# Linear attention and a gated convolution MoE on one core: keys' maximum as a bias in batch 0 only, later ranks for weights and MoE, other buffer counts, and six products on a zeroed tile first

## The chip, the cores and the metric

The kernel runs on one core of a Trainium2 chip. The metric is the device time of one execution in microseconds (us), the median of several runs. The core has five engines, each with its own list of instructions that it works off in order: TensorE (PE for products, PEld for the loads of their weights), VectorE (DVE), ScalarE (ACT), GpSimd (POOL) and SyncE (SP), which here issues every DMA. They wait for each other by semaphores alone.

## The reference

Eight batches with eight heads of 576 rows and 64 columns. Attention is linear: keys and queries are projected to 128 features, less the row's largest absolute value, and taken as exp(+) and exp(-). Its output, 512 wide for each row, goes through one feed-forward part with a convolution of three taps as gate.

```python
def phi(x):
    proj = np.einsum('bhsd,df->bhsf', x, w_phi)
    proj = proj - np.max(np.abs(proj), axis=-1, keepdims=True)
    return np.concatenate([np.exp(proj), np.exp(-proj)], axis=-1)
q_p, k_p = (phi(q), phi(k))
kv = np.einsum('bhsf,bhsd->bhfd', k_p, v)
z = np.sum(k_p, axis=2)
num = np.einsum('bhsf,bhfd->bhsd', q_p, kv)
den = np.einsum('bhsf,bhf->bhs', q_p, z)[..., None] + 1e-06
...
h = np.maximum(x @ w_in, 0.0)
...
gate = 1.0 / (1.0 + np.exp(-conv_out))
return (h * gate @ w_out).astype(np.float32)
```

Here x is the attention's output, w_in is 512 x 1024, w_out 1024 x 512, and conv_out the convolution of h along the rows. The three MoE weights come as float64.

## The kernel before

**Work and tiles.** Two heads lie side by side on the partitions, so a batch has two halves `qd` of four heads, each cut into five groups `g`: four of 256 columns for a pair of heads (n = 2, four row blocks of 128 in the end) and a short one for the last 64 rows of all four heads (n = 1). There are 80 key groups (`k_group`, line 418) and 80 query groups (`q_group`, line 460). Numbers that must keep float32's accuracy are split into a high and a low part in a faster format, and a product is made of three: high by high, high by low, low by high. The projections of batch 0's queries and of three key groups use plain float32 instead (`plain`, line 373).

**A key group.** `project` (line 370) loads it, splits it on POOL, projects it on PE into PSUM, and DVE takes the largest absolute value for each row and head block (line 404). For keys, ACT makes the negated maximum (line 407), and eight exponentials of 128 columns each read PSUM with the maximum, or its negative, as a bias (line 427; four in the short group). PE multiplies them with the values into `kv` (lines 441 and 445), in small tiles of 64 columns.

**A query group.** Here DVE subtracts the maximum from the whole group (line 411) into the SBUF tile `qs`, PE transposes it (line 469), ACT takes two exponentials of 512 columns (line 474), PE multiplies them by `kv` in small tiles (line 489), and DVE divides: the tile `x` (line 501).

**MoE.** Each pair of batches is cut into three chunks of 384 rows, twelve in all. `x_part` (line 509) transposes x and splits it, `h_part` (line 546) makes 8 blocks of h with 12 products each (line 562), relu on ACT, the convolution on POOL and DVE (lines 567 and 574) into the one tile `c`, the sigmoid, the gate's product (line 582) and its split into `gh` and `gl` (lines 591 and 594). `o_part` (line 598) makes four output blocks of 24 products (line 612). Chunk 0 needs the eight x tiles of batch 0 (g = 1 to 4 in both halves), chunk 1 four of them again, a short one of each half and four of batch 1, chunk 2 all of batch 1.

**Weights.** `load_weight` (line 340) loads a 128 x 512 piece of float64 words and rounds it by hand: in `float64_round` four DVE steps (lines 301, 306, 309, 316), two ACT steps (304, 313) and a POOL product (320), then a cast on ACT (362) and the low part on POOL (363). There are eight pieces of w_in, then eight of w_out. The raw words sit in the two slots `gh`, the half-made ones in the two slots `gl`, the same slots that the gate's tiles take later. Slots of a kind are given out in the order in which the program names their tiles, so every weight comes before the first gate tile. The first four blocks of h need pieces 0, 2, 4 and 6, which come first.

**The order.** A planner (`Plan`, line 88) writes the five lists. Each piece of work has an engine, a planned cost and hold, a rank, and the tiles that it reads, writes and takes. `order` (line 158) goes through planned time: it takes the work that can start earliest, and among those that can start at the same time the lowest rank. Work that needs a slot which isn't free can't start. Products in small tiles (`tiled`) are held back while PE has other work until four of them (`NT`) stand ready or one has waited 12 us; once PE has turned to them, it goes on with all that are ready.

**Ranks.** The chains are numbered: ten key groups of batch 0, then a query group of batch b and a key group of batch b+1 by turns, 160 in all. A key or query group has its number as its rank. Weight j of w_in has WIN0 + WIN x j, of w_out WOUT0 + WOUT x j, its DMA three less. Chunk n has M0 + 12.5 n + LEAD, that is 30 + 12.5 n.

**Buffers.** KE tiles of exponentials of keys (two per group), QE of queries (one per group), NXX tiles x of long groups (and four for the short ones), QS for `qs`, NHH for h. PSUM has four banks for general use, two (`M`) for h and output blocks (and batch 0's keys), two for `kv`.

Of the kernel before, what the change touches and what calls it, by code (L numbers as in the profile page):

```python
# [7 lines left out]
F32 = mybir.dt.float32  # L8
# [3 lines left out]
AF = mybir.ActivationFunctionType  # L12
# [4 lines left out]
F = 128  # L17
DM, FF = 512, 1024
P = 128
# [18 lines left out]
SWITCH = (120, 250)  # L38
TABLE = 1283
PSUM_G = 4  # L40
LEAD = 20
WIN0 = 0.0
WIN = 2.5
WOUT0 = 20.0
WOUT = 3.0
AGE = 12000.0
NT = 4
SLACK = 0.0
# [1 line left out]
RX = 0.0  # L50
OL = 0.0
KPLAIN = 3
KE = 6
NXX = 12
NHH = 10
TR = 2
QS = 2
QE = 3
V = 3
OS = 2  # L60
KVF = 6
# [165 lines left out]
def kernel(  # L227
# [13 lines left out]
    nc = tc.nc  # L241
# [6 lines left out]
    def piece(shape, dtype, name, tag, n=1):  # L248
        return Piece(sb, shape, dtype, name, [f"{tag}_{i}" for i in range(n)])

    def const(shape, dtype, name):
        return Piece(cp, shape, dtype, name, [name])

    G = [f"g_{i}" for i in range(PSUM_G)]
    M = [f"m_{i}" for i in range(2)]

    def psum(shape, name, slots):
        return Piece(pg, shape, F32, name, slots, True)
# [8 lines left out]
    def act(cost, hold, emit, reads, writes, rank, takes=(), table=None):  # L267
        plan.add("ACT", cost, hold, emit, reads, writes, rank, takes, table=table)

    def pool(cost, hold, emit, reads, writes, rank, takes=()):  # L270
        plan.add("POOL", cost, hold, emit, reads, writes, rank, takes)

    def mm(cost, emit, reads, writes, rank, takes=(), tiled=False):
        plan.add("PE", cost, cost, emit, reads, writes, rank, takes, tiled=tiled)

    def w_(*ps):
        return [p if isinstance(p, tuple) else (p, None) for p in ps]
# [11 lines left out]
    bias_e = const([P, 1], F32, "bias_e")  # L289
    pool(99, 60, lambda: nc.gpsimd.memset(bias_e(), -896.0 * (1 << 23)), (), w_(bias_e), -30)  # L290

    def float64_round(raw, w, power, n, rank, rraw, rw, rpower):


        def words():
            v = raw().rearrange("p (n two) -> p n two", two=2)
            return v[:, :, 0], v[:, :, 1]

        big = n > 100
        tcost = (700, 620) if big else (170, 95)  # L300
        vec(*tcost, lambda: nc.vector.tensor_scalar(out=w().bitcast(I32), in0=words()[1], scalar1=0x7FF00000, scalar2=None,
                                             op0=ALU.bitwise_and), rraw, rw, rank)
        act(*((722, 620) if big else (297, 190)),
            lambda: nc.scalar.activation(out=power().bitcast(I32), in_=w().bitcast(I32), func=AF.Relu, scale=8.0,
                                         bias=bias_e()), rw + w_(bias_e), rpower, rank + 0.01)
        vec(*tcost, lambda: nc.vector.tensor_scalar(out=w().bitcast(I32), in0=words()[1], scalar1=0xFFFFF, scalar2=0x100000,
                                             op0=ALU.bitwise_and, op1=ALU.bitwise_or), rraw, rw, rank + 0.02)
        vec(*((900, 820) if big else (700, 620)),
            lambda: nc.vector.scalar_tensor_tensor(out=power().bitcast(I32), in0=words()[1], scalar=-2147483648,
                                                   in1=power().bitcast(I32), op0=ALU.bitwise_and,  # L310
                                                   op1=ALU.bitwise_or), rraw + rpower, rpower, rank + 0.03)
        act(*((677, 570) if big else (210, 116)),
            lambda: nc.scalar.activation(out=words()[0].bitcast(F32), in_=words()[0].bitcast(U32), func=AF.Copy,
                                         scale=2.0**-52), rraw, [(p, "low") for p, _ in rraw], rank + 0.03)
        vec(*((930, 850) if big else (170, 95)),
            lambda: nc.vector.scalar_tensor_tensor(out=w(), in0=w().bitcast(I32), scalar=2.0**-20,
                                                   in1=words()[0].bitcast(F32), op0=ALU.mult, op1=ALU.add),
            rw + [(p, "low") for p, _ in rraw], rw, rank + 0.04)
        pool(*((1350, 1250) if big else (238, 200)),
             lambda: nc.gpsimd.tensor_tensor(out=w(), in0=w(), in1=power(), op=ALU.mult), rw + rpower, rw, rank + 0.05)  # L320
# [49 lines left out]
    def project(src, b, qd, g, kind, r):  # L370
        c0, n = group_columns(g)
        nm = f"{b}_{qd}_{g}"
        plain = kind == "q" and 2 * b + qd < NQ_F32 or kind == "k" and b == 0 and 5 * qd + g < KPLAIN
        raw = piece([P, n * P], F32, f"{kind}r{nm}", "th" if plain else "tr", TH if plain else TR)
        dma(lambda: raw(), lambda: src[b, qd, :, c0 : c0 + n * P], 64 * n, r - 3.0, writes=w_(raw))
        if not plain:
            hi = piece([P, n * P], F32R, f"{kind}xh{nm}", "th", TH)
            lo = piece([P, n * P], F32R, f"{kind}xl{nm}", "tl", TL)
            pool(*((407, 371) if n == 2 else (300, 265)),
                 lambda: nc.gpsimd.tensor_scalar(out=hi(), in0=raw(), scalar1=1.0, scalar2=0.0, op0=ALU.mult,  # L380
                                                 op1=ALU.add), w_(raw), w_(hi), r - 1.5)
            pool(*((735, 695) if n == 2 else (458, 420)),
                 lambda: nc.gpsimd.tensor_tensor(out=lo(), in0=raw(), in1=hi().bitcast(F32), op=ALU.subtract),  # L383
                 w_(raw, hi), w_(lo), r - 1.5)
        ps = psum([P, n * 256], f"{kind}p{nm}", M + G if b == 0 and kind == "k" else G)
        m = piece([P, 2, 2 * n], F32, f"{kind}m{nm}", "m", 6)
        pr = None if kind == "k" else piece([P, 2 * n, F], F32, f"qs{nm}", "qs", QS)

        def emit():
            for t in range(n):  # L390
                o = ps()[:, t * 256 : (t + 1) * 256]
                if plain:
                    nc.tensor.matmul(out=o, lhsT=raw()[:, t * P : (t + 1) * P], rhs=wbd_f(), start=True, stop=True)
                    continue
                his, los = hi()[:, t * P : (t + 1) * P], lo()[:, t * P : (t + 1) * P]
                nc.tensor.matmul(out=o, lhsT=his, rhs=wbd_hi(), start=True, stop=False)  # L396
                nc.tensor.matmul(out=o, lhsT=his, rhs=wbd_lo(), start=False, stop=False)  # L397
                nc.tensor.matmul(out=o, lhsT=los, rhs=wbd_hi(), start=False, stop=True)  # L398

        mm((432 if plain else 357) * n, emit, w_(raw, wbd_f) if plain else w_(hi, lo, wbd_hi, wbd_lo), w_(ps), r,  # L400
           takes=(m,) if pr is None else (m, pr))
        ps3 = lambda: ps().rearrange("p (t f) -> p t f", f=F)
        vec(*((690, 600) if n == 2 else (415, 331)),
            lambda: nc.vector.tensor_reduce(out=m()[:, 0], in_=ps3(), axis=AX, op=ALU.max, apply_absolute_value=True),  # L404
            w_(ps), [(m, 0)], r)
        if pr is None:
            act(200, 60, lambda: nc.scalar.activation(out=m()[:, 1], in_=m()[:, 0], func=AF.Copy, scale=-1.0), [(m, 0)],
                [(m, 1)], r)
            return n, ps, m
        vec(*((690, 600) if n == 2 else (415, 331)),  # L410
            lambda: nc.vector.tensor_tensor(out=pr(), in0=ps3(),
                                            in1=m()[:, 0].unsqueeze(2).broadcast_to([P, 2 * n, F]), op=ALU.subtract),
            [(ps, None), (m, 0)], w_(pr), r - 0.1)
        return n, pr

    kvps, kv = {}, {}

    def k_group(b, qd, g, r):
        n, ps, m = project(kT, b, qd, g, "k", r)
        nm = f"{b}_{qd}_{g}"  # L420
# [2 lines left out]
        dma(lambda: v(), lambda: vt[b, qd, :, v0 * VW : (v0 + 4) * VW], 130, r - 1.0, writes=w_(v))  # L423
        e = [piece([P, 2 * n, F], F32, f"ke{nm}_{s}", "ke", KE) for s in range(2)]
        for s in (1, 0):
            for i in range(2 * n):
                act(277, 160, lambda s=s, i=i: nc.scalar.activation(  # L427
                    out=e[s]()[:, i], in_=ps()[:, i * F : (i + 1) * F], func=AF.Exp, scale=1.0 - 2.0 * s,
                    bias=m()[:, 1 - s, i : i + 1]), [(ps, None), (m, 1 - s)], [(e[s], i)], r, table="Exp")
        if g == 0:  # L430
# [201 lines left out]
    for j, n in enumerate((0, 2, 4, 6, 1, 3, 5, 7)):  # L632
        load_weight(n, WIN0 + WIN * j)
    for j in range(8):
        load_weight(8 + j, WOUT0 + WOUT * j)
    rank_of = {}
# [5 lines left out]
    for n in range(NCH):  # L642
        r = M0 + step * n + LEAD
        x_part(n, r + RX)
        h_part(n, r)
        if n > 0:
            o_part(n - 1, r + 4.5 + OL)
    o_part(NCH - 1, M0 + step * NCH + LEAD + 4.5)

# [59 lines left out]
```

## Time and profile before

| what | us |
|---|---|
| median of 3 runs (lowest to highest) | 784.03 (783.07 to 784.82) |
| the profiled execution's own time | 784.47 |
| its span, first to last instruction | 782.7 |
| PE busy in the span | 751.4 |
| DVE, ACT, POOL busy | 500.2, 461.1, 286.3 |
| first product on PE starts | 5.81 |

The page gives for each engine the busy time, then the span in 40 equal slices with the busy share of each in tenths. The windows give the same for stretches that are chosen. The groups put together the instructions of one line, engine and operation: their tiles, how many, their busy time, the mean time of one, and the idle time before them. Products on PE overlap, so that their busy time hides how close they follow each other; the timeline gives the starts. The chain of waits goes back from the last instruction to what released each step.

### The profile page before, as it was taken

What the parts mean: (1) busy time and instruction counts of PE and PEld (TensorE: products, weight loads), DVE (VectorE), ACT (ScalarE), POOL (GpSimd) and SP (SyncE); (2) the same over time, 40 slices, a digit from 0 to 9 for tenths busy, and PEclk for the clock granted to TensorE, in tenths of its full rate; (3) what the DMA queues carried; (4) which work ended last, traced back from release to release, by engine and by line L of the source; (5) the groups of instructions that cost most, each with busy time, mean ns of one, the idle gap of its engine ahead of it and who ended that gap; (6) DMA issues with size and microseconds to landing.
All of it is one profiled execution on the core that took longest, in us unless ns stands there. A gap on an engine that the chain in (4) does not pass through costs nothing.

```text
span 782.7 us, 20365 instructions
## 1 busy us (share of the span) xinstructions
PE 751.4 (96%) x8265; PEld 720.7 (92%) x8265; DVE 500.2 (64%) x1030; ACT 461.1 (59%) x1172; POOL 286.3 (37%) x428
## 2 busy tenths in 40 slices
PE   6888888999999999999999999999999999999998
PEld 5777887899999999999999999999999999999997
DVE  4898788755566655666756665666555757766550
ACT  6998748665547727646647654736654763733341
POOL 4877675422252412433512341423332434220110
PEclk9999999999999999999999999999999999999999
DMA  5655311112202311220311221201310220000001
GB/s 176 198 154 153 108 56 45 48 32 75 72 21 58 86 38 46 69 56 32 89 33 56 58 62 35 79 22 35 107 43 25 85 70 21 29 12 22 21 21 50
DMA packets 46604, 48.88 MB, mean 62 GB/s; under 512 B 5296, under 2 KB 44464, under 8 KB 46512
## 3 DMA queue, kind: packets, MB, share of 16 engines
q1 hardware_dynamic: 46512, 47.59, 20.6%
q8 instruction: 65, 1.06, 0.6%
q14 instruction: 27, 0.22, 0.1%
HBM read 38.13 MB, written 9.44 MB: 61 GB/s over the span
## 4 chain that ended last, share of the span: by engine, by line
PE 76%; ACT 11%; DVE 9%; POOL 2%; issue 1%; DMA 1%; SPq 0%; POOLq 0%; ACTq 0%
PE hp L562 24%; PE op L612 23%; PE nm L489 8%; ACT ke L427 6%; PE kv L445 6%; PE tp L469 4%; PE xt L532 2%; DVE c L574 2%; PE qp L396 2%; PE qp L398 2%; PE qp L397 1%; PE kp L396 1%; PE kp L398 1%; PE kp L397 1%; PE kv L441 1%; DVE km L404 1%
## 5 line engine op out<-in xcount | busy, mean ns | idle before, releaser
L574 DVE SCALAR_TENSOR_TENSOR c<-h,cw,c 128x384 f32<-128x384 f32 (+3 forms) x256 | 139.2, 575 | 69.1 <-POOL c L567 67.7
L427 ACT ACTIVATE ke<-kp,km 128x128 f32<-128x128 f32 x576 | 163.0, 416 | 2.1 <-PE kv L445 2.1
L562 PE MATMUL hp<-xh,win_hi 128*128 128x386 f32 x384 | 134.5, 350 | 0.4 <-ACT h L566 0.3
L612 PE MATMUL op<-gh,wout_hi 128*128 128x384 f32 x384 | 131.9, 343 | 0.0
L562 PE MATMUL hp<-xl,win_hi 128*128 128x386 f32 x384 | 131.4, 342 | 0.0
L562 PE MATMUL hp<-xh,win_lo 128*128 128x386 f32 x384 | 131.1, 341 | 0.0
L567 POOL TENSOR_SCALAR c<-h,cw 128x384 f32<-128x384 f32 x96 | 61.0, 636 | 190.0 <-ACT h L566 189.0
L612 PE MATMUL op<-gl,wout_hi 128*128 128x384 f32 x384 | 130.0, 338 | 0.0
L612 PE MATMUL op<-gh,wout_lo 128*128 128x384 f32 x384 | 129.5, 337 | 0.0
L566 ACT ACTIVATE h<-hp 128x386 f32<-128x386 f32 x96 | 47.7, 499 | 131.8 <-PE hp L562 130.9
L474 ACT ACTIVATE qe<-tp 128x512 f32<-128x512 f32 (+1 forms) x160 | 81.2, 571 | 36.2 <-PE tp L469 35.9
L383 POOL TENSOR_TENSOR qxl<-qr,qxh 128x256 fp32r<-128x256 f32 (+1 forms) x70 | 54.5, 779 | 121.2 <-PE qp L398 118.8
L383 POOL TENSOR_TENSOR kxl<-kr,kxh 128x256 fp32r<-128x256 f32 (+1 forms) x77 | 60.1, 781 | 80.3 <-PE kp L398 76.6
L489 PE MATMUL nm<-kvf,qe 128*64 128x65 f32 (+1 forms) x2304 | 86.3, 229 | 1.5 <-ACT qe L474 1.1
L489 PEld LDWEIGHTS nm<-kvf,qe 128*64 128x64 f32 x2304 | 78.0, 137 | 8.4 <-issue 4.3
L404 DVE TENSOR_REDUCE qm<-qp 128x4 f32<-128x512 f32 (+1 forms) x80 | 50.6, 633 | 41.8 <-PE qp L398 40.2
L445 PE MATMUL kv<-v,ke 128*64 128x65 f32 x2048 | 75.0, 223 | 1.8 <-ACT ke L427 1.8
L562 PEld LDWEIGHTS hp<-xh,win_hi 128*128 128x128 f32 x384 | 73.5, 191 | 2.6 <-ACT h L566 0.9
L404 DVE TENSOR_REDUCE km<-kp 128x4 f32<-128x512 f32 (+1 forms) x80 | 50.5, 632 | 38.7 <-PE kp L398 33.1
L562 PEld LDWEIGHTS hp<-xl,win_hi 128*128 128x128 f32 x384 | 73.2, 191 | 0.8 <-DVE xl L540 0.8
L445 PEld LDWEIGHTS kv<-v,ke 128*64 128x64 f32 x2048 | 68.3, 137 | 5.8 <-ACT ke L427 2.4
L562 PEld LDWEIGHTS hp<-xh,win_lo 128*128 128x128 f32 x384 | 73.4, 191 | 0.0
(71 smaller groups left out, 1414.1 us busy)
## 6 DMA issues: line engine op xcount, KB each, us to landing
v<-in_vt_dram SPq DMA_DIRECT2D x80, 130.0 KB, 2.3
kr<-in_kT_dram SPq DMA_DIRECT2D x64, 128.0 KB, 2.1
qr<-in_qT_dram SPq DMA_DIRECT2D x64, 128.0 KB, 2.1
out_dram<-os SPq DMA_DIRECT2D x32, 192.0 KB, 1.9
w_r<-in_w_in_dram SPq DMA_DIRECT2D x8, 512.0 KB, 4.1
w_r<-in_w_out_dram SPq DMA_DIRECT2D x8, 512.0 KB, 3.5
out_dram<-os SPq DMA_DIRECT2D x32, 96.0 KB, 1.7
kr<-in_kT_dram SPq DMA_DIRECT2D x16, 64.0 KB, 1.8
```

Source lines behind the costliest of these rows:

```text
L383: lambda: nc.gpsimd.tensor_tensor(out=lo(), in0=raw(), in1=hi().bitcast(F32), op=ALU.subtract),
L404: lambda: nc.vector.tensor_reduce(out=m()[:, 0], in_=ps3(), axis=AX, op=ALU.max, apply_absolute_value=True),
L427: act(277, 160, lambda s=s, i=i: nc.scalar.activation(out=e[s]()[:, i], in_=ps()[:, i * F : (i + 1) * F], func=AF.Exp, scale=1.0 - 2.0 * s ...
L445: nc.tensor.matmul(out=kp[i]()[a : a + 64, s, p0 : p0 + VW], lhsT=lhsT, rhs=v()[:, (2 * t + i) * VW : (2 * t + i + 1) * VW], start=False, ...
L469: nc.tensor.transpose(out=tp()[:, i, t, :], in_=pr()[:, 2 * t + i, :], identity=idn())
L474: lambda s=s: nc.scalar.activation(out=qe()[:, s], in_=tp(), func=AF.Exp, scale=1.0 - 2.0 * s),
L489: nc.tensor.matmul(out=ps()[a : a + 64, t, i, :], lhsT=qe()[:, s, i, t, a : a + 64], rhs=kv[b, qd][i]()[:, s, p0 * VW : p0 * VW + w], star ...
L562: nc.tensor.matmul(out=ps(), lhsT=w, rhs=x, start=(p == 0 and k == 0), stop=(p == 3 and k == 2))
L566: act(494, 373, lambda ps=ps, hs=hs: nc.scalar.activation(out=hs(), in_=ps(), func=AF.Relu), w_(ps), w_(hs), rf)
L567: pool(590, 557, lambda f=f, hs=hs: nc.gpsimd.tensor_scalar(out=c4()[:, f, :], in0=hs()[:, o : o + TC], scalar1=cwv()[:, f, 1:2], scalar2= ...
L574: lambda f=f, hs=hs, j=j, lo=lo, hi=hi: nc.vector.scalar_tensor_tensor(out=c4()[:, f, lo:hi], in0=hs()[:, o + j - 1 + lo : o + j - 1 + hi] ...
L612: nc.tensor.matmul(out=ps(), lhsT=w, rhs=x, start=(i == 0), stop=(i == 23))
```

## The change

Keys take the maximum as a bias only in the batches of `KB`, which is batch 0. For the others `project` subtracts it on DVE as it does for queries, into one of two SBUF tiles `ks` (`KS`), the negated maximum isn't made, and two exponentials over the whole group take the place of eight. The planned time of a biased exponential goes from 277 and 160 ns (cost and hold) to 393 and 250, that of the negated maximum from 200 and 60 to 207 and 95.

LEAD goes from 20 to 36, so chunk n has the rank 46 + 12.5 n. Weights of w_in have the ranks 0, 5, ... 35 instead of 0, 2.5, ... 17.5; those of w_out 50, 54, ... 78 instead of 20, 23, ... 41. KE goes from 6 to 4, QE from 3 to 2, NXX from 12 to 14. And a tile of 128 x 128 is zeroed by POOL and multiplied by itself six times on PE, in plain float32, with the lowest rank of all, into a PSUM tile that nothing reads.

```diff
-LEAD = 20
+LEAD = 36
 WIN0 = 0.0
-WIN = 2.5
-WOUT0 = 20.0
-WOUT = 3.0
+WIN = 5.0
+WOUT0 = 50
+WOUT = 4.0
...
-KE = 6
-NXX = 12
+WARM = 6
+KB = (0,)
+KS = 2
+KE = 4
+NXX = 14
...
-QE = 3
+QE = 2
...
+    if WARM:
+        blank = const([P, P], F32, "blank")
+        pool(150, 110, lambda: nc.gpsimd.memset(blank(), 0.0), (), w_(blank), -31)
+        spare = psum([P, P], "spare", M)
+        for i in range(WARM):
+            mm(430, lambda: nc.tensor.matmul(out=spare(), lhsT=blank(), rhs=blank(), start=True, stop=True), w_(blank),
+               w_(spare), -31)
...
-        pr = None if kind == "k" else piece([P, 2 * n, F], F32, f"qs{nm}", "qs", QS)
+        biased = kind == "k" and b in KB
+        pr = None if biased else piece([P, 2 * n, F], F32, f"{kind}s{nm}", kind + "s", KS if kind == "k" else QS)
...
-            act(200, 60, lambda: nc.scalar.activation(out=m()[:, 1], in_=m()[:, 0], func=AF.Copy, scale=-1.0), [(m, 0)],
+            act(207, 95, lambda: nc.scalar.activation(out=m()[:, 1], in_=m()[:, 0], func=AF.Copy, scale=-1.0), [(m, 0)],
                 [(m, 1)], r)
             return n, ps, m
...
-        return n, pr
+        return (n, pr) if kind == "q" else (n, pr, None)
...
         for s in (1, 0):
+            if m is None:
+                act(*((630, 522) if n == 2 else (416, 307)),
+                    lambda s=s: nc.scalar.activation(out=e[s](), in_=ps(), func=AF.Exp, scale=1.0 - 2.0 * s),
+                    w_(ps), w_(e[s]), r, table="Exp")
+                continue
             for i in range(2 * n):
-                act(277, 160, lambda s=s, i=i: nc.scalar.activation(
+                act(393, 250, lambda s=s, i=i: nc.scalar.activation(
```

## The prediction

> **What bounds the kernel now.** I read the page's busy shares and slices first, then the windows of the stages, then the chain of waits of one stage, then the groups of instructions in the first 160 us.
>
> ```profile
> PE 751.4 (96%) x8265; PEld 720.7 (92%) x8265; DVE 500.2 (64%) x1030; ACT 461.1 (59%) x1172; POOL 286.3 (37%) x428
> ...
> PE   6888888999999999999999999999999999999998
> ...
> DVE  4898788755566655666756665666555757766550
> ACT  6998748665547727646647654736654763733341
> ```
> ```profile
> 0.00:40.00 40.00, 30.46 (x371) 24.70 (x372) 26.80 (x42) 33.15 (x111) 25.51 (x36) 1.00 0.61 187
> 40.00:80.00 40.00, 33.64 (x606) 28.88 (x606) 35.38 (x74) 36.69 (x106) 27.20 (x29) 1.00 0.53 156
> 80.00:120.00 40.00, 35.83 (x319) 33.56 (x313) 34.14 (x62) 22.56 (x58) 28.77 (x29) 0.91 0.23 70
> 120.00:160.00 40.00, 35.58 (x484) 33.07 (x484) 30.47 (x65) 28.27 (x69) 18.26 (x27) 0.96 0.19 53
> 160.00:680.00 520.00, 516.77 (x5731) 502.99 (x5730) 320.81 (x672) 304.24 (x769) 174.22 (x288) 1.00 0.19 53
> 680.00:760.00 80.00, 80.00 (x664) 78.90 (x663) 48.94 (x115) 30.66 (x54) 12.31 (x21) 1.00 0.06 19
> 760.00:782.70 22.70, 19.16 (x109) 18.61 (x107) 3.65 (x4) 5.50 (x9) 0.00 (x0) 1.00 0.13 47
> ```
>
> The columns after the length are the busy times of PE, PEld, DVE, ACT and POOL, then the granted clock. There are two kernels here. From 160 us on, PE is busy 516.77 of 520 us, and the end is one stream of products: nothing that speeds another engine pays there. Before 160 us, PE is busy 135.5 us of 160, ACT 36.69 of 40 between 40 and 80 us, DVE 35.38 and 34.14 of 40 between 40 and 120 us. The change can only earn in that head.
>
> Busy PE understates the loss, since a lone product counts with its whole latency. So I price the work itself.
>
> ```profile
> 774.10 0.34 PE L612 MATMUL op<-gl,wout_hi 128*128 128x384 f32 x1
> ...
> 774.27 0.34 PE L612 MATMUL op<-gh,wout_hi 128*128 128x384 f32 x1
> ```
> ```profile
> L612 PE MATMUL op<-gh,wout_hi 128*128 128x384 f32 x293 | 101.1, 345 | 0.0
> ...
> L562 PE MATMUL hp<-xh,win_hi 128*128 128x386 f32 x268 | 92.9, 347 | 0.4 <-ACT h L566 0.3
> ...
> L489 PE MATMUL nm<-kvf,qe 128*64 128x65 f32 (+1 forms) x1568 | 60.1, 230 | 0.4 <-ACT ke L427 0.4
> ```
> ```profile
> L445 PE MATMUL kv<-v,ke 128*64 128x65 f32 x672 | 28.3, 228 | 1.8 <-ACT ke L427 1.8
> ...
> L562 PE MATMUL hp<-xh,win_lo 128*128 128x386 f32 x52 | 18.9, 364 | 0.0
> ...
> L489 PE MATMUL nm<-kvf,qe 128*64 128x65 f32 (+1 forms) x512 | 18.2, 226 | 1.1 <-ACT qe L474 1.1
> ...
> L441 PE MATMUL kv<-v,ke 128*64 128x130 f32 x96 | 7.2, 296 | 0.1
> ```
>
> The first fence is the timeline: MoE products start 0.175 us apart. The second is the groups of 160 to 680 us: some 1,683 MoE products (each of the two rows has two sister rows of the same count) take 295 us at that pace; the other 225 us of the 520 hold 1568/2304 of the 80 query groups, 54, and about as many key groups. A pair of a key and a query group thus costs PE 4.1 us. The third is the groups of 0 to 160 us: 672/32 + 96/16 = 27 key groups, 512/2304 x 80 = 18 query groups, 156 products of the first MoE part. At the dense prices that is 18 x 4.1 + 9 x 2.05 + 156 x 0.175 = 120 us of work in 160. **The head loses some 40 us**, of which 5.8 pass before the first data land (row of L393 below).
>
> What held it is in the chain of waits from 38.5 to 160 us:
>
> ```profile
> by line: PE hp L562 11.6%; ACT ke L427 9.8%; DVE c L574 9.7%; ACT qe L474 5.5%; PE kv L445 5.0%; DVE w_t L309 3.9%; issue 3.5%; PE tp L469 3.5%; DVE w_t L306 3.3%; DVE w_t L316 3.3%; PE nm L489 3.2%; POOL w_t L320 3.1%; DVE km L404 3.0%; AC
> ```
>
> Of 121.5 us, the keys' exponentials (L427) hold 9.8%, 11.9 us, and the four printed steps of the weights' conversion 13.6%, 16.5 us. Those two are what the change touches.
>
> **The change part by part.** Groups of ACT, DVE and POOL in 0 to 160 us:
>
> ```profile
> L427 ACT ACTIVATE ke<-kp,km 128x128 f32<-128x128 f32 x192 | 56.1, 462 | 0.0
> L474 ACT ACTIVATE qe<-tp 128x512 f32<-128x512 f32 (+1 forms) x36 | 18.8, 588 | 11.5 <-PE tp L469 11.4
> L313 ACT ACTIVATE w_r<-w_r 128x512 f32<-128x512 uint32 x16 | 12.7, 791 | 0.0
> L304 ACT ACTIVATE w_t<-w_t,bias_e 128x512 int32<-128x512 int32 x16 | 12.4, 794 | 1.5 <-DVE w_t L301 1.5
> ...
> L411 DVE TENSOR_TENSOR qs<-qp,qm 128x512 f32<-128x512 f32 (+1 forms) x18 | 11.7, 651 | 0.1
> ```
>
> *Keys of batches 1 to 7.* An exponential with a bias costs ACT 56.1/192 = 0.29 us, a group of eight 2.34. Two over 512 columns cost 2 x 18.8/36 = 1.04, and the negated maximum goes too. DVE gains one subtraction, 0.65 us (11.7/18). Over the run ACT loses about 504 x 0.283 - 126 x 0.52 = 77 us, DVE gains about 70 x 0.62 = 43 us and rises from 64% to 69%. After 160 us both lie beside PE's work: nothing. In the head 17 of the 27 key groups change. On the chain 11.9 us become 11.9 x 1.04/2.34 = 5.3: **-6.6**; the subtraction returns where a group is on the chain, five groups (11.9/2.34) by 0.65: **+3.3**. Bounds: nothing to -6.6 for the one; for the other 0 to 17 x 0.65 = +11, if DVE is the bound everywhere.
>
> ```profile
> L316 DVE SCALAR_TENSOR_TENSOR w_t<-w_t,w_r x16: 656/786/1780, 12.5 to 115.0; 128x512 f32<-128x512 int32 x16
> ...
> L363 POOL TENSOR_TENSOR wout_lo<-w_t,wout_hi x8: 1257/1292/1854, 65.5 to 117.8; 128x512 fp32r<-128x512 f32 x8
> ```
> ```profile
> L411 DVE TENSOR_TENSOR qs<-qp,qm x80: 409/679/693, 34.6 to 713.0; 128x512 f32<-128x512 f32 x64, 128x256 f32<-128x256 f32 x16
> ```
>
> A DVE step of the weights swings from 0.66 to 1.78 us here; the queries' subtraction never passes 0.693, so 0.65 stands. The Trainium skill (SBUF — State Buffer, "Who interferes with whom") says that a DVE instruction with two SBUF inputs and a GpSimd instruction that reads SBUF exclude each other, one with a single SBUF input not; the new subtraction has one, in PSUM its other. By the opposite, each could cost 1.78 and the term be 5.6 higher.
>
> *Weights later (WIN, WOUT0, WOUT).* A rank decides only between works that could start at the same time, so no work vanishes: 16 conversions stay. In the first 38 us keys of batch 0 keep ACT full. Ranks below their ten chains belong to weights 0 to 9.99/2.5, four; then to two. Two less delay batch 0's keys by 2 x (12.7 + 12.4)/16 and a cast that I take like L313, 0.8: 2 x 2.4 = 4.8 us of ACT; I take **-4** (bounds 0 to -4.8, since keys' projections wait for DMA there too). Behind it, up to 160 us, weights stand behind attention that has work: I take half of their 16.5 us on the chain, **-8** (bounds 0 and -16.5), the half that can be filled by attention. Of each weight, the DMA issue (SP), five DVE and ACT steps and two POOL steps move together. The two slots of raw words are shared with the gate's tiles, so the gate of chunk 0 now waits for weight 15. Behind its copy on ACT's list stand exponentials, and behind those PE's small-tile products; PE has attention meanwhile, as long as x has room (rival c).
>
> *LEAD, NXX.* MoE's rank moves 16 chains back; with 14 tiles of x, batch 0's eight and six of batch 1's go ahead of the first transposition instead of four. More attention before the first MoE product, the same sum: 0 by itself (bounds: -4.1, two more query groups of 2.05 brought into PE's pauses; to +8.2, two pairs of 4.1 that DVE can't feed).
>
> *Planned costs.* The order is written from planned times, and each engine keeps to it. The plan held 0.16 us for a biased exponential that takes 0.29 in the head: 192 x 0.13 = 25 us of ACT that it did not know of. After, it is 72 x 0.04 = 3. What PE's list gains from that no row shows; I take 0 (bounds 0 and -11, a third of the head's 34 us beyond the first data) and let it speak for rival (a).
>
> *KE 6 to 4, QE 3 to 2, KS.* At most four small-tile works can now stand ready, the number that the planner asks for before it turns PE's mode. Those batches of at most four instead of six mean some more turns, and projections that wait for a buffer: **+2** (bounds 0 and +6; no row prices it, the nearest is the ACT ke wait of 1.8 us in L445's row, which I round up).
>
> *Six products on zeros.*
>
> ```profile
> L393 PE MATMUL qp<-wbd_f,qr 128*128 128x256 f32 x36 | 10.1, 398 | 5.1 <-ACT ke L427 2.2 <-ACT qe L474 1.6 <-DMA qr<-in_qT_dram 1.0
> ...
> L393 PE MATMUL kp<-wbd_f,kr 128*128 128x256 f32 x10 | 4.6, 647 | 5.8 <-DMA kr<-in_kT_dram 5.8
> ```
>
> The first ten full-precision products of the kernel take 647 ns each, later ones of the same shape 398, though the granted clock reads 1.00 in both. At 0.46 us per record of 256 columns (4.6/10) and two records a product, six of half the width take about 6 x 0.46 = 2.8 us, and lie inside the 5.8 us of waiting: 0. If they did bring the faster state, ten records would save 10 x 0.21 = 2 us, most of it ahead of an ACT that is full anyway; bounds 0 and -2. The Trainium skill (TensorE: Matmul & The Clock Gate, "What's actually happening") asks for some 3.4 us of sustained work before the clock is released; 2.8 us with a pause behind them fall short, and by that rule the term is 0 too.
>
> **Sum**: -6.6 + 3.3 - 4 - 8 + 2 = -13.3. The profiled span of 782.7 becomes 769.4. The profiled execution took 784.47, 1.8 outside its span, the median is 784.03, 1.3 above the span: I say **771**.
>
> **Rivals.**
> (a) *The head becomes dense* (chance 0.17): ACT, freed, feeds PE all through. For it: the clock of 0.91 and 0.96 between 80 and 160 us comes from PE's pauses and gives some 5 us back; then both weights' terms are whole, and the sum is -6.6 + 3.3 - 4.8 - 16.5 and the zeros' -2, -26.6: 757.
> (b) *DVE takes ACT's place* (0.09): at 35.38 of 40 us it has little room, and 17 x 0.65 = 11 us come on top. With +11 for +3.3 and +6 for +2 the sum is -1.6, no change: 782.5.
> (c) *The second weights come too late* (0.18): no output product can start, and chunk 1 not be gated, before weight 15 is converted. Now that is at 119 us (L363 above), and eight take 7.5 us each. x has room for batches 0 and 1 and six of batch 2, 26 query groups with the short ones; they are eight beyond the 18 of 160 us, done at some 190 us. If three weights are then open, PE stands for 3 x 7.5 = 22 us, and the sum is +9: 793. It decides from two open weights on. Against it: the planner lets idle DVE take them earlier.
> (d) *The ranks change nothing* (0.06): work starts when it can. Only the exponentials' -6.6 + 3.3 + 2 remain: 782.7.
>
> **How the numbers follow.** My forecast, 0.50, covers 763 to 779. Faster, by over 0.2% (1.6 us, about what a measurement of this kernel tells from none): 0.50 + 0.17 + a third of (b) and (d), 0.05: 0.72. Same: the rest of (b) and (d): 0.10. Slower: (c), 0.18. The range leaves out the better part of (a) and the worse half of (c): 757 to 788.
>
> **What would show it.**
>
> ```profile
> L562 PE MATMUL hp<-xh,win_hi x384: 332/338/672, 87.3 to 748.9; 128*128 128x386 f32 x192
> ```
>
> Right: the first MoE product of chunk 0 (now at 87.3 us) starts by 80 us; ke falls to 72 + 140 instructions and ACT to some 370 us busy; PE in 0 to 160 us has some 13 us more work; its busy share after 160 us is unchanged; PE stops at most 1.8 us ahead of kv for ke. (a) shows as a clock of 1.00 from 80 us on. Wrong: DVE over 37 of 40 us from 40 to 160 us with pauses on PE (b); wout_lo's last conversion past 180 us with PE idle before the first op (c); the first ten products at 400 ns would show that the zeros worked.

## The result, and the profile after

The changed kernel takes 763.22 us (median of 4 runs, 761.96 to 765.37), the one before 783.74: a ratio of 0.974 (95% interval 0.9712 to 0.9768), 20.5 us less. The forecast was 771, between 757 and 788; the result lies at the fast edge of the band of 763 to 779 that the prediction gave to its own theory. The profiled execution took 765.37 us; its span is 763.6 us, 19.1 less than before. This is the page's first part and the slices of the kernel after:

```profile
PE 744.7 (98%) x8277; PEld 719.2 (94%) x8277; DVE 536.1 (70%) x1100; ACT 392.5 (51%) x738; POOL 280.7 (37%) x429
...
PE   7999989999999999999999999999999999999998
...
DVE  4699999689886595576775766766866677475540
ACT  6877557644734554543463563562553453534331
```

and these are its windows (busy PE, PEld, DVE, ACT, POOL, granted clock, DMA):

```profile
0.00:40.00 40.00, 35.20 (x465) 30.12 (x467) 23.03 (x44) 31.48 (x108) 20.94 (x36) 0.96 0.58 166
40.00:80.00 40.00, 38.15 (x647) 34.47 (x643) 39.45 (x86) 29.01 (x59) 25.63 (x33) 1.00 0.51 154
80.00:120.00 40.00, 36.87 (x449) 35.30 (x449) 38.82 (x71) 24.77 (x41) 28.38 (x36) 0.96 0.32 94
120.00:160.00 40.00, 37.57 (x429) 35.81 (x427) 33.22 (x62) 25.16 (x51) 25.63 (x32) 1.00 0.30 88
160.00:680.00 520.00, 516.81 (x5839) 503.98 (x5839) 363.80 (x765) 254.81 (x443) 171.32 (x283) 1.00 0.18 51
```

Between 40 and 80 us ACT falls from 36.69 to 29.01 of 40, and DVE rises from 35.38 to 39.45: the engine that is nearly full in the head is now DVE, which hardly pauses from 40 to 120 us, and no longer ACT. PE is busier in each of the four windows, and after 160 us as before (516.81 of 520). The groups of PE in 0 to 160 us tell the work:

```profile
L462 PE MATMUL kv<-v,ke 128*64 128x65 f32 x736 | 25.4, 224 | 0.0
L579 PE MATMUL hp<-xh,win_hi 128*128 128x386 f32 x64 | 21.9, 342 | 0.0
...
L506 PE MATMUL nm<-kvf,qe 128*64 128x65 f32 (+1 forms) x544 | 19.4, 226 | 0.6 <-DVE x L518 0.6
...
L458 PE MATMUL kv<-v,ke 128*64 128x130 f32 x96 | 6.6, 278 | 0.0
L405 PE MATMUL kp<-wbd_f,kr 128*128 128x256 f32 x10 | 4.5, 638 | 1.3 <-DMA kr<-in_kT_dram 1.3
L629 PE MATMUL op<-gh,wout_hi 128*128 128x384 f32 x7 | 2.4, 336 | 0.0
```

That is 736/32 + 96/16 = 29 key groups, 544/2304 x 80 = 19 query groups and 192 + 20 MoE products (the rows of the other two parts have 64, 64, 7 and 6). At the prediction's dense prices it is 19 x 4.1 + 10 x 2.05 + 212 x 0.175 = 135.5 us, against 120 before. By this estimate 15.5 of the 19.1 us come from the first 160 us. The same count, called dense work below, is taken for other runs and other times.

### The profile page after: what moved, and what is told of

Its sections match the earlier page's. It is cut to its first block, busy times and chain, and to the rows that moved or that the text cites. A ratio compares the mean times of both kernels' runs of the same rounds, so it can differ in the third digit from the quotient of the medians.

```text
span 763.6 us, 20198 instructions
## 1 busy us (share of the span) xinstructions
PE 744.7 (98%) x8277; PEld 719.2 (94%) x8277; DVE 536.1 (70%) x1100; ACT 392.5 (51%) x738; POOL 280.7 (37%) x429
## 4 chain that ended last, share of the span: by engine, by line
PE 78%; DVE 12%; POOL 4%; ACT 3%; issue 2%; DMA 0%; SPq 0%; POOLq 0%; ACTq 0%
PE op L629 24%; PE hp L579 22%; PE nm L506 8%; PE kv L462 5%; PE tp L486 4%; DVE c L591 3%; PE xt L549 2%; PE kp L408 2%; PE kp L410 2%; PE kp L409 2%; PE qp L408 1%; PE qp L410 1%; PE qp L409 1%; DVE c L599 1%; PE kv L458 1%
## 5 line engine op out<-in xcount | busy, mean ns | idle before, releaser
L579 PE MATMUL hp<-xh,win_hi 128*128 128x386 f32 x384 | 132.6, 345 | 0.0
L579 PE MATMUL hp<-xl,win_hi 128*128 128x386 f32 x384 | 129.6, 338 | 0.0
L440 ACT ACTIVATE ke<-ks 128x512 f32<-128x512 f32 (+1 forms) x140 | 76.4, 598 | 63.0 <-DVE ks L423 39.2
L491 ACT ACTIVATE qe<-tp 128x512 f32<-128x512 f32 (+1 forms) x160 | 78.4, 563 | 47.3 <-PE tp L486 46.9
L394 POOL TENSOR_TENSOR kxl<-kr,kxh 128x256 fp32r<-128x256 f32 (+1 forms) x77 | 58.4, 759 | 94.2 <-PE kp L410 91.2
L394 POOL TENSOR_TENSOR qxl<-qr,qxh 128x256 fp32r<-128x256 f32 (+1 forms) x70 | 51.2, 732 | 108.9 <-PE qp L410 106.7
L611 DVE TENSOR_TENSOR gl<-c,gh 128x768 fp32r<-128x768 f32 x48 | 47.0, 1013 | 36.4 <-ACT gh L608 35.9
L629 PEld LDWEIGHTS op<-gh,wout_hi 128*128 128x128 f32 x384 | 72.1, 188 | 0.2 <-issue 0.2
L629 PEld LDWEIGHTS op<-gl,wout_hi 128*128 128x128 f32 x384 | 72.1, 188 | 0.2 <-DVE gl L611 0.2
L629 PEld LDWEIGHTS op<-gh,wout_lo 128*128 128x128 f32 x384 | 72.2, 188 | 0.0
```

What stands on the lines that cost most here:

```text
L440: lambda s=s: nc.scalar.activation(out=e[s](), in_=ps(), func=AF.Exp, scale=1.0 - 2.0 * s),
L491: lambda s=s: nc.scalar.activation(out=qe()[:, s], in_=tp(), func=AF.Exp, scale=1.0 - 2.0 * s),
L579: nc.tensor.matmul(out=ps(), lhsT=w, rhs=x, start=(p == 0 and k == 0), stop=(p == 3 and k == 2))
L611: vec(1000, 920, lambda f=f, a=a, gh4=gh4, gl4=gl4: nc.vector.tensor_tensor(out=gl4()[:, a : a + 2, :], in0=c4()[:, f : f + 2, :], in1=gh4 ...
L629: nc.tensor.matmul(out=ps(), lhsT=w, rhs=x, start=(i == 0), stop=(i == 23))
```

## The experiments

Each run is compared with the kernel before on the same chip, so the ratios are what can be set side by side; one thousandth is 0.78 us. The changed kernel ran again, with no edit, on the same chip as three of its variants (old planned costs, order held without the zeros, old ranks of the weights):

> The changed kernel itself, beside its variants on the same chip: 762 to 765 us.

764.34 us, ratio 0.974 (0.972 to 0.976), as in the result.

**One part undone at a time.** Keys' maximum as a bias in every batch:

```diff
-KB = (0,)
+KB = tuple(range(8))
```

> The changed kernel, but with the maximum as a bias in all eight batches (KB = 0 to 7): no subtraction of keys on DVE, eight exponentials again; ranks, buffers and zeros as changed. The forecast's theory (later weights bring most of the 20.5 us, the subtraction a net 3.3): 766 to 769 us, ACT near 460 us busy. Rival (ACT's relief brings most): 776 to 784 us, with ACT full between 20 and 80 us as before.

769.25 us, ratio 0.9807 (0.9792 to 0.9821), at the upper end of the forecast's theory, with ACT 459 us busy. Window of 40 to 80 us:

```profile
40.00:80.00 40.00, 38.41 (x612) 34.30 (x611) 37.45 (x81) 37.65 (x114) 26.18 (x34) 1.00 0.48 144
```

ACT is as full as it was in the kernel before (37.65 of 40), and yet PE is busy 38.41 us instead of 33.64. So in this window ACT's relief is not what fills PE. DVE is at 37.45 us here without any subtraction of keys, so that its rise from 35.38 isn't the subtraction's alone either.

The old buffers (with one tile `ks`, so that they fit, which is an edit of its own):

```diff
-KS = 2
-KE = 4
-NXX = 14
+KS = 1
+KE = 6
+NXX = 12
...
-QE = 2
+QE = 3
```

> The changed kernel with the buffers of before (KE 6, QE 3, NXX 12), and KS 1 so that it fits. The forecast's theory (fewer buffers cost 2 us): 759 to 763 us. Rival (the two more x tiles carry the attention's lead and so the gain): 768 to 775 us.

769.24 us, ratio 0.98 (0.9777 to 0.9823): the rival's time, and the forecast's theory missed. The old buffers bring no 2 us back; what they cost or bring by themselves this run can't say, as will be seen below.

The old planned costs:

```diff
-            act(207, 95, lambda: nc.scalar.activation(out=m()[:, 1], in_=m()[:, 0], func=AF.Copy, scale=-1.0), [(m, 0)],
+            act(200, 60, lambda: nc.scalar.activation(out=m()[:, 1], in_=m()[:, 0], func=AF.Copy, scale=-1.0), [(m, 0)],
...
-                act(393, 250, lambda s=s, i=i: nc.scalar.activation(
+                act(277, 160, lambda s=s, i=i: nc.scalar.activation(
```

> The changed kernel with the planned costs of before for batch 0's biased exponentials and the negated maximum (277 and 160, 200 and 60). Same work, another order. The forecast (planned costs count nothing): 763 to 766 us. Rival (an order planned with too short an ACT stalls PE in the first 40 us): 768 us or more, with less PE work by 40 us.

769.12 us, ratio 0.9798 (0.978 to 0.9816). That is the rival's time, and PE is busy 32.66 us of the first 40 against 35.20 (34.51 in the changed kernel's second run). But only the order differs here, and below stand orders with these costs right that take as long.

No products on zeros:

```diff
-WARM = 6
+WARM = 0
```

> The changed kernel without the six products on zeros. The forecast's theory (they bring nothing): 762.5 to 764 us. Rival (they release the clock for the first ten products, which PE then does 2 us faster): 765 us, with the first ten products 427 ns apart instead of some 217.

768.56 us, ratio 0.9791 (0.9773 to 0.9809), above both. The first ten products start 427 ns apart, as the rival has it, but so they do in the profiled execution of the result, with the zeros.

**Four parts, four times the same answer.** Bias, buffers, costs, zeros: each undone alone gave 0.979 to 0.981. This is suspicious, because each of these edits also makes the planner write another order on every engine. Three runs test that. In the first, the order is the changed kernel's on all five engines, and only the six products aren't issued:

```diff
-            mm(430, lambda: nc.tensor.matmul(out=spare(), lhsT=blank(), rhs=blank(), start=True, stop=True), w_(blank),
+            mm(430, lambda: None, w_(blank),
                w_(spare), -31)
```

> The changed kernel's own order on every engine, with only the six products on zeros left out (their place in the plan stays). Theory after the run without them (the plan made without them is another order, and that cost most of the 4 to 5 us): 762 to 765 us, at most 1 us over the changed kernel. Rival (the zeros themselves bring 4 us by the clock): 767 to 769 us.

765.38 us, ratio 0.9749 (0.9732 to 0.9767), with the changed kernel's 0.974 inside the interval: not the rival's time. So most of what the run without zeros lost is the order's. In the other two the work is the same, and a planned time is off by a few nanoseconds:

```diff
-TAIL = 165
+TAIL = 170
```

> The changed kernel with TAIL 170 instead of 165: products are planned 5 ns longer, nothing else; the work is the same, the order on PE another. Theory after eight runs (any other order costs some 4 us, so that the 4 to 5 us of biased exponentials, old buffers and old planned costs say nothing of these parts): 767 to 771 us. Rival (the order is not that delicate, and those parts are worth 4 to 5 us each): 762 to 765.5 us.

```diff
-SLACK = 0.0
+SLACK = 3.0
```

> The changed kernel with SLACK 3 instead of 0: PE is planned 3 ns later behind other engines, nothing else. As with the run before: 767 to 771 us if any other order costs some 4 us, 762 to 765.5 us if not.

770.74 us, ratio 0.9826 (0.9808 to 0.9843), and 767.01 us, ratio 0.9772 (0.9756 to 0.9789). So **an order made from times that mean nothing costs 2.5 to 6.7 us** ((0.9772 - 0.974) and (0.9826 - 0.974) times 784); the interval of the smaller one just touches the changed kernel's, that of the larger one is clear of it. The four single edits lie inside that. None of them can be told from a new order. For the planned costs and these two edits the order is all that differs, so there the changed kernel just has an order that fits better; for the bias and the buffers, how much is the order's stays open. A window of TAIL 170 and one of SLACK 3 show where such an order loses:

```profile
40.00:80.00 40.00, 35.62 (x613) 32.52 (x609) 36.96 (x83) 29.05 (x58) 25.18 (x31) 1.00 0.50 145
```
```profile
120.00:160.00 40.00, 32.58 (x397) 30.34 (x395) 36.42 (x73) 24.68 (x44) 23.44 (x29) 0.91 0.28 84
```

The changed kernel has PE busy 38.15 and 37.57 us there. The pauses fall in different places. SLACK 3 has 129 us of dense work by 160 us, against 135.5. TAIL 170 has made up its loss by then (134.7) and loses again later: from 160 to 680 us PE is busy 513.96 us, against 516.81. In SLACK 3 PE's longest waits between 5 and 200 us (sum, count, longest) are for the queries' subtraction:

```profile
PE nm L506 <- DVE qs L423: 4.3, 2, 2.2
PE tp L486 <- DVE qs L423: 3.1, 3, 2.1
```

In TAIL 170 the longest are for the division's tile `x` instead (3.0 us in three waits). DVE is busy 36 to 37 of 40 us in both windows, and PE stops where the work at the front of its list is one that DVE still owes.

**The ranks.** All back, then the weights' alone, then LEAD alone:

```diff
-LEAD = 36
+LEAD = 20
...
-WIN = 5.0
-WOUT0 = 50
-WOUT = 4.0
+WIN = 2.5
+WOUT0 = 20.0
+WOUT = 3.0
```

> The changed kernel with the ranks of before (LEAD 20, WIN 2.5, WOUT0 20, WOUT 3): weights and MoE early again, keys still subtracted on DVE. The forecast's theory: most of the gain is lost, 775 to 782 us, first MoE product later than 80 us. Rival (ACT's relief brings most): 763 to 769 us.

780.68 us, ratio 0.9952 (0.9936 to 0.9969): nearly the whole gain is gone, as the forecast's theory has it. But the first MoE product starts at 73.0 us, not after 80, so a late start of MoE is not what takes the gain.

```diff
-WIN = 5.0
-WOUT0 = 50
-WOUT = 4.0
+WIN = 2.5
+WOUT0 = 20.0
+WOUT = 3.0
```

> The changed kernel with the weights' ranks of before (WIN 2.5, WOUT0 20, WOUT 3), LEAD stays 36. The forecast's theory (the weights stood on the chain, LEAD by itself is worth nothing): 776 to 781 us, as with all old ranks. Rival (LEAD is what counts): 763 to 768 us.

770.53 us, ratio 0.9826 (0.9796 to 0.9856): between the two, and no more than the new order with TAIL 170. The head does show what early weights take: by 80 us this run has done 17 key groups, 8 query groups and 6 MoE products, 52 us of dense work, the changed kernel 20, 10 and 15, 64 us, and the two orders of no meaning 62. Of these 12 us, 9.5 are left at 160 us and 7.6 at 680.

```diff
-LEAD = 36
+LEAD = 20
```

> The changed kernel with LEAD 20, weights late as changed. The forecast's theory (LEAD by itself is worth nothing): 763 to 767 us. Rival (early MoE ranks take DVE and PE from the attention that should run ahead, worth the 10 us between old weights' ranks and all old ranks): 772 to 776 us.

777.7 us, ratio 0.9914 (0.9898 to 0.993). That is more than even the rival said. **LEAD carries the most**: 13.6 us against the changed kernel, 7 to 11 against its two orders of no meaning, which are but two. The weights' ranks are worth 3 us more below it (0.9952 - 0.9914), which is no more than an order can make.

Stretches of LEAD 20 show how. Its windows, then the changed kernel's:

```profile
80.00:100.00 20.00, 17.59 (x171) 17.09 (x170) 19.97 (x33) 9.05 (x18) 13.95 (x14) 1.00 0.24 69
100.00:125.00 25.00, 20.02 (x223) 18.99 (x223) 23.04 (x40) 15.46 (x23) 16.09 (x22) 0.80 0.26 78
```
```profile
80.00:100.00 20.00, 19.90 (x246) 19.26 (x246) 19.78 (x38) 12.05 (x23) 13.53 (x19) 1.00 0.33 99
100.00:125.00 25.00, 21.98 (x273) 20.87 (x273) 24.04 (x43) 17.71 (x30) 18.37 (x22) 0.93 0.34 102
```

From 80 to 100 us DVE is full in both (19.97 and 19.78 of 20), so the difference is what it works on, and in which order. With LEAD 20 chunk 0 has a lower rank than the attention of that time; its convolutions come first on DVE, and the attention's subtractions wait behind. PE's timeline, then DVE's, of LEAD 20:

```profile
105.40 1.09 PE L486 MATMUL tp<-idn,qs 128*128 128x128 f32 x4 [2.15 <-DVE qs L423]
107.41 0.55 PE L408 MATMUL qp<-wbd_hi,qxh 128*128 128x256 f32 x1 [0.92 <-DVE xl L557]
107.76 0.42 PE L409 MATMUL qp<-wbd_lo,qxh 128*128 128x256 f32 x1
```
```profile
103.91 0.74 DVE L591 SCALAR_TENSOR_TENSOR c<-h,cw,c 128x383 f32<-128x383 f32 x1
104.58 0.68 DVE L423 TENSOR_TENSOR qs<-qp,qm 128x512 f32<-128x512 f32 x1
105.18 1.01 DVE L591 SCALAR_TENSOR_TENSOR c<-h,cw,c 128x384 f32<-128x384 f32 x1
```

PE waits 2.15 us for a subtraction whose maximum was made at 102.36 us (0.68 us), and which stood behind two convolutions of 1.70 us together, the second of them in the first row. PE's waits of 5 to 200 us, LEAD 20 first and then the changed kernel, have the sums of this wait:

```profile
PE tp L486 <- DVE qs L423: 9.8, 4, 3.6
```
```profile
PE tp L486 <- DVE xl L557: 3.4, 3, 2.4
...
PE tp L486 <- DVE qs L423: 0.3, 1, 0.3
```

In the changed kernel the same transpositions wait 3.4 us for another work of DVE, the split of x.

After the two pauses of LEAD 20 that its timeline shows, 2.15 and 0.92 us, PE's products take 0.42 us in place of 0.28, and the clock of 100 to 125 us is 0.80. The longest of the four waits, 3.6 us, comes at 179 us; from 160 to 200 us PE is busy 35.75 us there, against 38.35. By dense work LEAD 20 is 3 us behind at 160 us (133 against 135.5) and 11 at 680 (642 against 653.5), so by this estimate more is lost after the head than in it.

The last stretch is the end. The same two kernels, 680 to 755 us:

```profile
680.00:720.00 40.00, 37.74 (x408) 35.97 (x407) 25.60 (x72) 18.18 (x30) 7.07 (x11) 1.00 0.02 7
720.00:755.00 35.00, 34.24 (x200) 33.73 (x201) 20.38 (x39) 12.95 (x21) 4.69 (x8) 1.00 0.07 23
```
```profile
680.00:720.00 40.00, 40.00 (x236) 39.96 (x235) 25.00 (x56) 15.70 (x25) 6.46 (x10) 1.00 0.06 20
720.00:755.00 35.00, 35.00 (x201) 34.78 (x200) 12.76 (x21) 10.58 (x15) 2.35 (x4) 1.00 0.11 35
```

and when the division makes the first and the last tile x, in LEAD 20, the kernel after and the one before:

```profile
L518 DVE TENSOR_TENSOR x<-nm,rc x96: 273/423/426, 34.7 to 722.2; 128x256 f32<-128x256 f32 x64, 64x128 f32<-64x128 f32 x32
```
```profile
L518 DVE TENSOR_TENSOR x<-nm,rc x96: 273/417/426, 34.5 to 681.1; 128x256 f32<-128x256 f32 x64, 64x128 f32<-64x128 f32 x32
```
```profile
L501 DVE TENSOR_TENSOR x<-nm,rc x96: 273/424/425, 46.2 to 724.9; 128x256 f32<-128x256 f32 x64, 64x128 f32<-64x128 f32 x32
```

With LEAD 20 attention lasts to 722 us, and PE pauses 3.0 us there (40 - 37.74 + 35 - 34.24). With LEAD 36 it is over at 681 us, and MoE alone fills PE. The kernel before also ended late, but without a pause; it had one more buffer of exponentials for a query group and one more pair for a key group. That these buffers spared it the pause was not tried.

**The ranks without the rest.** The kernel before, with the new ranks only:

```diff
-LEAD = 20
+LEAD = 36
...
-WIN = 2.5
-WOUT0 = 20.0
-WOUT = 3.0
+WIN = 5.0
+WOUT0 = 50
+WOUT = 4.0
```

> The kernel before with the changed ranks alone (LEAD 36, WIN 5, WOUT0 50, WOUT 4); biased keys, buffers, planned costs as before, no zeros. The forecast's theory (later weights -12): 770 to 775 us. Rival (ranks pay only with the subtraction on DVE, since ACT is full): 779 to 785 us.

779.72 us, ratio 0.9942 (0.9927 to 0.9956): 4.5 us. The rival's time. The same ranks undone in the changed kernel cost 16.6 us. So the ranks pay in full only beside something else. It is not the subtraction alone, for with all keys biased the changed kernel still has 0.9807, and not the buffers or the planned costs alone. The run with all keys biased and this one both have biased keys and new ranks and lie 10.6 us apart (0.9942 - 0.9807), more than any order of no meaning cost; what differs are the planned costs, the buffers and the zeros. Planned costs of 0.16 us for exponentials that take 0.29 count for 576 of them here and for 72 in the run with the old costs, so they are the likelier cause; but no run tried it, and it stays open.

## Why the prediction was right, and where its sum was not

**Where the time would come from** held. 15.5 us of the 19.1 lie in the first 160 us, and PE's share after them is unchanged. The first MoE product starts at 64.3 us (forecast: by 80, before 87.3). Biased exponentials are 72, whole ones 140; ACT is at 392.5 us, not 370: the exponentials saved 66.5 us (163.0 before, 20.1 + 76.4 after), not 77. PE's row of L462 shows no wait for an exponential in the first 160 us. PE has 15.5 us more work by 160 us (forecast: some 13). These rows of the kernel after carry the exponentials and the first MoE product:

```profile
L440 ACT ACTIVATE ke<-ks 128x512 f32<-128x512 f32 (+1 forms) x140 | 76.4, 598 | 63.0 <-DVE ks L423 39.2 <-PE kv L458 10.1 <-PE kv L462 9.3
...
L444 ACT ACTIVATE ke<-kp,km 128x128 f32<-128x128 f32 x72 | 20.1, 456 | 0.0
```
```profile
L579 PE MATMUL hp<-xh,win_hi x384: 332/338/447, 64.3 to 725.5; 128*128 128x386 f32 x192
```

**LEAD at 0** is the term that failed. Its bounds were -4.1 to +8.2; it is worth -7 to -11 us against orders of no meaning, outside them. I had counted only how many query groups x has room for, and reasoned that the same sum of work remains. A rank also decides whose work goes first on the engine that is full, DVE; and it decides whether attention or MoE is left over at the end.

**Later weights at -12** (-4 and -8) was too much: 3 us with LEAD 20, and with LEAD 36 the 6.7 us of the ratio (0.9826 - 0.974); neither exceeds what a meaningless order costs. The forecast looked at the first half only. With LEAD 20 the later weights put 9 us more dense work before 80 us (66.6, against 57.3 with all old ranks), and at 680 us half a microsecond is left of it (642.3 against 641.8). With LEAD 36 it is 12 and 7.6 us. That fits conversions that are only moved and are paid for later, which no run tests by itself. Taking the weights' steps off the chain of waits didn't shorten the kernel by their length.

**The exponentials at -6.6 + 3.3** can't be confirmed or refuted: undone they cost 5.2 us (0.9807 - 0.974), within the scatter of orders. **The buffers at +2** can't be told either.

**The sum is nearer than its terms.** -13.3 against a measured -19.1 looks like a good sum, but its largest term, -12 for the weights, was too much, and LEAD, at 0, was too little by about as much, if the runs above are taken at their word. That the two errors offset each other is luck.

**The zeros at 0** are within reach: 0.7 us by the ratios with the order held, intervals overlapping. But the reason, that they always fall short, was wrong. PE's timeline in the first microseconds, in the profiled execution of the result, in that of the same kernel's second run, and with the products left out:

```profile
0.99 2.93 PE L300 MATMUL spare<-blank 128*128 128x128 f32 x12 [0.99 <-POOL bias_e L293]
5.23 4.51 PE L405 MATMUL kp<-wbd_f,kr 128*128 128x256 f32 x10 [1.31 <-DMA kr<-in_kT_dram]
```
```profile
0.99 2.93 PE L300 MATMUL spare<-blank 128*128 128x128 f32 x12 [0.99 <-POOL bias_e L293]
5.44 2.60 PE L405 MATMUL kp<-wbd_f,kr 128*128 128x256 f32 x10 [1.51 <-DMA kr<-in_kT_dram]
```
```profile
5.21 4.20 PE L405 MATMUL kp<-wbd_f,kr 128*128 128x256 f32 x10 [5.21 <-DMA kr<-in_kT_dram]
```

The zeros take 2.93 us, where 2.8 were estimated. In one execution the ten products after them still take 4.51 us, in the other 2.60, and the 1.9 us between them are the 2 us of the bound. Over all profiled executions with zeros, the ten take 2.47 and 2.60 us in two and 3.81 to 4.61 us in eight; in the four without zeros, 4.20 to 4.61 us. So the clock is released early in some executions and not in most. The Trainium skill (TensorE: Matmul & The Clock Gate, "What's actually happening") says that the window of 3.4 us runs freely and doesn't start with the kernel. That the outcome changes between executions fits it. The 3.4 us of sustained work that the same section asks for don't fit: twice 2.93 us and a pause were enough, and there the measurement decides.

**The rivals.** (a) came half: the clock between 80 and 160 us rose from 0.91 and 0.96 to 0.96 and 1.00, and the result lies nearer to its 757 than to 771. But its reason, an ACT set free, is not what filled PE from 40 to 80 us. (b) was half right: DVE did take ACT's place as the engine that is full (39.45 and 38.82 of 40 us), and yet PE is busier than it was with DVE at 88% and ACT at 92%. (c) did not decide: the last weight's low part starts at 161.3 us, and PE is busy 37.57 of the 40 us up to 160, with attention. (d) is refuted by the 16.6 us of the ranks.

**The order itself** was not in the sum. I had looked at it only as wrong planned costs and put it at 0. The changed kernel's order is 2.5 to 6.7 us better than those of its two neighbours, which lie at 767 and 771; the forecast was 771. So an order that happens to fit can be most of what the measurement has beyond the forecast, and the prediction had no term for that.

## What to carry to other kernels

Where a program writes out the order from planned times, try an edit of no meaning, such as a planned time off by some nanoseconds, before a few microseconds are put down to an edit of meaning; and hold the order fixed to price an instruction. When a bound moves from one engine to another, ask which of the waiting works the new bound takes first: a rank that looks neutral in sums decides it. A step that stands on the chain of waits need not be worth its length, as the weights' steps here were not; work that is put off has to be counted where it lands.

## What the runs showed of the hardware

The granted clock of the windows doesn't show the slow first products: they have 1.00 for 5 to 10 us of the kernel before, while its ten records of L393 take 647 ns each, and later records of the same shape 398. The starts show it: 426 to 427 ns apart where the ten take 4.61 us, 216 where they take 2.60. The trace of the kernel before has no record of its clock at all before 11.6 us, where the first release stands.

Products on zeros do count for the clock. Where the ten products take 2.47 and 2.60 us, the trace has the first release of the clock at 4.4 us, after the zeros and before any other product; in the other eight executions with zeros it comes at 8.1 to 11.9 us, and in the four without at 8.9 to 11.6 us.

A short pause was followed by a slower clock: in LEAD 20 PE's pause of 2.15 us begins at 103.25 us, the trace has the clock at one half from 105.0 to 111.8 us, and products take 0.42 us instead of 0.28 until 111.7 us.
